# One weight load cut by partitions, and vector work spread over three engines, in a decode step that streams 91 MB

## The chip, the cores and the metric

One core of a Trainium2 chip. The metric is device time in microseconds. The kernel before takes 220.0 us (median of three runs, 219.9 to 220.01).

## The reference

One decode step for two sequences (B = 2). Grouped-query attention with 32 query heads over 8 key/value heads looks at the last W = 4096 positions of the caches; beside it runs a dense layer with the Mish activation; a sigmoid gate mixes the two. Everything is float32.

```python
g = sigmoid((x * gate_w).sum(-1))                      # x: [2, 1, 512]
q = x @ wq                                             # wq: 512 x 4096
p = softmax(q k^T * 128 ** -0.5)                       # per head, 4096 positions
a = (p v) @ wo                                         # wo: 4096 x 512
h = x @ w1 + b1                                        # w1: 512 x 1792
b = (h * tanh(softplus(h))) @ w2                       # w2: 1792 x 512
out = g * a + (1 - g) * b
```

## The kernel before

**The stream.** All large data arrives through one DMA queue, issued by SyncE (SP), in the order wq (two loads of 4 MB), w1, then k and v of the eight key/value heads in turn (4 MB each), and last the first ten blocks of w2 (`w2_0`, 2.5 MB), wo in four loads (`wo0`, `wo4`, `wo6`, `wo7`: four, two, one and one heads' worth) and the last four blocks of w2 in three (`w2_10` with two blocks, 512 KB, then `w2_12` and `w2_13` with one each, 256 KB). Each load is a tile of 128 partitions: a row of every partition is one packet, 32 KB for k and v, 4 KB for `w2_10`, 2 KB for `w2_12` and `w2_13`. All but the three last go through the pool `stream` with five buffers (`load`, line 54); those three have tiles of their own (`load_w2`, line 262). A stream load waits on SP until its buffer is free, and what follows it in the queue waits behind it.

**The attention.** TensorE works in column groups of 32: the two queries sit in 32-row blocks (Q = 32), and the four groups j hold four slices of the positions. For each head `softmax` (lines 128 to 144) makes 128x512 scores in `sc`, VectorE takes the row maximum (`mx`, line 134), ScalarE the exponentials with their row sums (`p`, `ls`), TensorE transposes p, and a copy brings it to SBUF (`pT`, line 143). `values` (line 146) multiplies pT with v into `o` and adds its four blocks, weighted by the 0/1 columns of `pick`, into `od` (lines 154 and 156). Each slice keeps its own maximum; only after the last head does `weights` (line 159) find the common one, turn the differences into factors (`ms`, lines 163 to 175), and make `kf` (factors by slice and head) and `r` (gate over the sum). `outputs` (line 194) then multiplies od with kf and writes the scaled, transposed heads to `oT`.

**The dense layer.** `hidden` (line 203) computes h early, after the queries, and the Mish in 14 small vector operations and one exponential, into `actT`.

**The end.** `project` (line 278) accumulates `w2_0` and wo into `acc`, in the four column groups: the columns of the result are the same in all groups, so that they must still be added. After the last wo pass ScalarE copies the left half of `acc` to `asum`, VectorE the right half (lines 306 and 307). `finish` (line 288) collects the result in `fin`: the two blocks of `w2_10` (`output(1)`), `asum` folded over its four groups by the matrix `fold`, then `w2_12` and `w2_13`. VectorE copies fin to `res` and SP stores it (lines 319 and 320).

A float32 matmul appears in the trace as two passes, each with a weight load. The framework (Tile) sets semaphores and buffers, and may put independent instructions of an engine in another order than the source.

## Time and profile before

| | |
|---|---|
| median of three runs | 220.0 us |
| profiled execution | 219.93 us, of which the span is 218.1 us |
| granted TensorE clock, mean | 0.797 |
| read from HBM | 91.24 MB, 419 GB/s over the span |
| TensorE busy (passes, weight loads) | 131.8 us, 39.3 us |
| VectorE, ScalarE, POOL busy | 36.2, 8.6, 3.0 us |
| VectorE instructions | 131 |

The span begins with the first instruction and ends with the last; the rest of the 219.93 us lies around it. Rows of a timeline have start, duration, engine, source line, operation, tiles and count, and in brackets the idle time before with what ended it. Rows of a table by stretch have, per engine, busy time and count, in the order PE, PEld, DVE, ACT, POOL; then the granted clock, the mean busy share of the 16 DMA engines and GB/s. A group's row has busy time and mean ns of one.

### The profile page before, as it was taken

To read this page: it belongs to the slowest core of one execution; us is meant where nothing else is said; L and a number is where in the kernel's file an instruction comes from. 1 tells how busy PE (TensorE), PEld (TensorE's weight loads), DVE (VectorE), ACT (ScalarE), POOL (GpSimd) and SP (SyncE) were. 2 spreads that over 40 slices of the span, in tenths; PEclk is the share of its full clock that TensorE was granted. 3 is DMA by queue.
4 is the path that set the end of the run, shared out by engine and by line. 5 is a ranking of instruction groups with operands and counts; after the bars stand their busy time and mean duration, and the time that the engine had idled before them with its cause. 6 is when DMAs were issued, how large, how long until landed. Compare 5 with 4: busy or idle time off the path is not lost.

```text
span 218.1 us, 1883 instructions
## 1 busy us (share of the span) xinstructions
PE 131.8 (60%) x798; PEld 39.3 (18%) x798; DVE 36.2 (17%) x131; ACT 8.6 (4%) x21; POOL 3.0 (1%) x9
## 2 busy tenths in 40 slices
PE   0057637295763828435684937467394946496975
PEld 0012212012111201201121112112021211341222
DVE  1012112402202021120112012011202023503001
ACT  2000000001001000100100010010001001000000
POOL 5000000000000000000000000000000000000000
PEclk9999988766669696995858787885858579758799
DMA  7998999999999999999999999999999999999993
GB/s 288 391 477 385 442 430 466 397 464 403 463 403 463 406 457 403 463 403 463 403 460 403 463 409 457 415 457 409 454 409 457 409 457 399 439 433 436 413 408 117
DMA packets 4183, 91.41 MB, mean 419 GB/s; under 512 B 592, under 2 KB 720, under 8 KB 1104
## 3 DMA queue, kind: packets, MB, share of 16 engines
q1 hardware_dynamic: 4176, 91.31, 97.6%
q8 instruction: 6, 0.10, 0.2%
q14 instruction: 1, 0.01, 0.0%
HBM read 91.24 MB, written 0.07 MB: 419 GB/s over the span
## 4 chain that ended last, share of the span: by engine, by line
DMA 80%; PE 16%; DVE 1%; SPq 1%; issue 1%; ACT 1%; DVEq 0%
DMA k<-in_kt 40%; DMA w<-in_w 20%; DMA v<-in_v 20%; PE o L150 5%; PE sc L131 5%; PE hp L209 2%; PE ol L196 1%; PE fin L288 1%; SPq L54 1%; ACT p L138 0%; PE lp L186 0%; DVE mx L134 0%; DVE pT L143 0%; PE pp L142 0%; DVE r L189 0%
## 5 line engine op out<-in xcount | busy, mean ns | idle before, releaser
L131 PE MATMUL sc<-k,qz 128*32 128x512 f32 x256 | 44.9, 866 | 32.2 <-DMA k<-in_kt 32.2
L150 PE MATMUL o<-v,pT 128*32 128x512 f32 x256 | 46.1, 886 | 10.2 <-DMA v<-in_v 8.4
L131 PEld LDWEIGHTS sc<-k,qz 128*32 128x32 f32 x256 | 10.1, 152 | 66.9 <-DMA k<-in_kt 39.6
L150 PEld LDWEIGHTS o<-v,pT 128*32 128x32 f32 x256 | 11.9, 153 | 38.0 <-issue 32.7
L134 DVE TENSOR_REDUCE mx<-sc 128x1 f32<-128x512 f32 x8 | 5.5, 692 | 63.1 <-PE sc L131 63.1
L113 PE MATMUL qp<-wqa,x 128*32 128x512 f32 x32 | 6.2, 710 | 13.3 <-DVE xg L93 13.3
L142 PE MATMUL pp<-ident,p 128*128 128x128 f32 x32 | 5.5, 295 | 14.4 <-ACT p L138 14.4
L154 DVE TENSOR_SCALAR od<-o,pick 128x128 f32<-128x128 f32 x8 | 2.8, 351 | 51.2 <-PE o L150 51.2
L138 ACT ACTIVATE p<-sc,bias 128x512 f32<-128x512 f32 x8 | 5.5, 687 | 140.2 <-DVE bias L136 122.7
L278 PE MATMUL acc<-wo,oT 128*32 128x512 f32 x64 | 8.8, 614 | 1.7 <-DMA wo<-in_wo 1.7
L156 DVE SCALAR_TENSOR_TENSOR od<-o,pick,od 128x128 f32<-128x128 f32 x24 | 8.4, 351 | 0.9
L143 DVE COPY pT<-pp 128x512 f32<-128x512 f32 x8 | 5.5, 692 | 11.7 <-PE pp L142 11.7
L142 PEld LDWEIGHTS pp<-ident,p 128*128 128x128 f32 x32 | 3.4, 142 | 21.1 <-ACT p L138 21.1
L209 PE MATMUL hp<-w,x 128*32 128x512 f32 (+1 forms) x32 | 5.0, 730 | 3.4 <-DMA w<-in_w 3.4
L196 PE MATMUL ol<-kf,od 128*128 128x8 f32 x16 | 3.5, 351 | 2.3 <-DVE od L156 1.6
L278 PE MATMUL acc<-w,actT 128*32 128x512 f32 x20 | 4.5, 914 | 0.0
L113 PE MATMUL qp<-wqb,x 128*32 128x512 f32 x32 | 3.6, 594 | 1.3 <-DMA wqb<-in_wq 1.3
L113 PEld LDWEIGHTS qp<-wqa,x 128*32 128x32 f32 x32 | 1.2, 128 | 15.7 <-DVE x L80 13.3
L196 PEld LDWEIGHTS ol<-kf,od 128*128 128x128 f32 x16 | 3.4, 312 | 3.5 <-DVE od L156 2.6
L278 PEld LDWEIGHTS acc<-wo,oT 128*32 128x32 f32 x64 | 2.4, 113 | 7.2 <-issue 5.6
L307 DVE COPY asum<-acc 128x256 f32<-128x256 f32 x1 | 0.4, 425 | 13.6 <-ACT asum L306 13.6
L116 DVE COPY qs<-qp 128x512 f32<-128x512 f32 x2 | 1.4, 692 | 7.7 <-PE qp L113 7.7
(75 smaller groups left out, 33.3 us busy)
## 6 DMA issues: line engine op xcount, KB each, us to landing
k<-in_kt SPq DMA_DIRECT2D x8, 4096.0 KB, 42.2
v<-in_v SPq DMA_DIRECT2D x8, 4096.0 KB, 43.0
wqa<-in_wq SPq DMA_DIRECT2D x1, 4096.0 KB, 12.2
wqb<-in_wq SPq DMA_DIRECT2D x1, 4096.0 KB, 21.0
wo<-in_wo SPq DMA_DIRECT2D x1, 4096.0 KB, 38.4
w<-in_w SPq DMA_DIRECT2D x1, 3584.0 KB, 29.1
w<-in_w SPq DMA_DIRECT2D x1, 2560.0 KB, 38.6
wo<-in_wo SPq DMA_DIRECT2D x1, 2048.0 KB, 33.3
```

The lines of the kernel that those rows point to most:

```text
L113: nc.tensor.matmul(qp[Q * k : Q * k + Q, :], x32[:, c, :], w[:, c, k, :], start=(c == 0), stop=(c == DC - 1))
L131: nc.tensor.matmul(sc[Q * j : Q * j + Q, :], qz[:, kv, m * Q : m * Q + Q], t[:, (m * NJ + j) * 512 : (m * NJ + j + 1) * 512], start=(m == ...
L134: nc.vector.tensor_reduce(mx[:, kv : kv + 1], sc, axis=AX.X, op=ALU.max)
L138: nc.scalar.activation(p, sc, AF.Exp, bias=bias, scale=SCALE, accum_out=ls[:, kv : kv + 1])
L142: nc.tensor.transpose(pp[:, c, :], p[:, c * P : (c + 1) * P], ident)
L143: nc.vector.tensor_copy(pT, pp)
L150: nc.tensor.matmul(o[Q * j : Q * j + Q], pT[:, c, Q * j : Q * j + Q], t[:, (c * NJ + j) * 512 : (c * NJ + j + 1) * 512], start=(c == 0), s ...
L154: nc.vector.tensor_scalar_mul(d, o[:, 0, :], pick[:, 0:1])
L156: nc.vector.scalar_tensor_tensor(d, o[:, m, :], pick[:, m : m + 1], d, op0=ALU.mult, op1=ALU.add)
L196: nc.tensor.matmul(ol[:, kv].rearrange("p b h -> p (b h)"), od[:, kv, :], kf[:, kv, :], start=True, stop=True)
L209: nc.tensor.matmul(hp[Q * j : Q * j + Q, :n], x32[:, c, :], w[:, c, j * FG * P : j * FG * P + n], start=(c == 0), stop=(c == DC - 1))
L278: nc.tensor.matmul(acc[Q * j : Q * j + Q, :], lhsT, rhs, start=(n_col[j] == 0), stop=(n_col[j] == n - 1))
```

## The change

`w2_10` is loaded in three DMAs of 81, 32 and 15 partitions instead of one of 128. [...] The three last w2 tiles get a pool of their own, `ends`, placed behind `stream`, which is now the first pool and starts at a multiple of 1024 bytes (`res` is padded for it).

VectorE's program becomes shorter, 47 instructions by the title:

- the constants and the spread x (`fold`, `key`, `ones`, `x32`), the products for the gate, two of its steps, most of the Mish and the last factor of `r` move to POOL;
- the copies of `qs`, `pT`, `ms` and `hs` move to ScalarE, and the scale goes into the copy of qs, so that the maximum can be stored negated and used as the bias of the exponential at once;
- many small operations become one over a larger pattern (`qz`, `mj`, `h`, the subtraction in `weights`, the product in `outputs`);
- `values` gathers two heads in one PSUM tile and makes od for both with one product and one sum;
- the Mish becomes h * e(e + 2) / (e(e + 2) + 2) with e = exp(min(h, 20));
- the sum over the gate's four chunks goes into TensorE's accumulation, four matmuls for one.

Since od now comes in pairs, the first `outputs` covers six heads instead of seven and the second two instead of one. `pT` has one buffer instead of two, and `o` takes two PSUM banks.

The diff, cut to its core:

```diff
+CAP = 20.0
 CUTS = (0, 10, 12, 13, 14)
+PARTS = (0, 81, 113, 128)
...
+    stream = ctx.enter_context(tc.tile_pool(name="stream", bufs=5))
+    ends = ctx.enter_context(tc.tile_pool(name="ends", bufs=1))
     const = ctx.enter_context(tc.tile_pool(name="const", bufs=1))
-    stream = ctx.enter_context(tc.tile_pool(name="stream", bufs=5))
+    single = ctx.enter_context(tc.tile_pool(name="single", bufs=1))
...
-        xs = const.tile([P, B], F32, name="xs")
-        nc.vector.tensor_reduce(xs, xg.rearrange("p c b -> p b c"), axis=AX.X, op=ALU.add)
         zp = ps_1.tile([P, B], F32, tag="q", name="zp")
-        nc.tensor.matmul(zp, ones, xs, start=True, stop=True)
+        for c in range(DC):
+            nc.tensor.matmul(zp, ones, xg[:, c, :], start=(c == 0), stop=(c == DC - 1))
...
-        nc.vector.tensor_reduce(mx[:, kv : kv + 1], sc, axis=AX.X, op=ALU.max)
-        bias = tiny.tile([P, 1], F32, tag="bias", name=f"bias{kv}")
-        nc.vector.tensor_scalar_mul(bias, mx[:, kv : kv + 1], -SCALE)
+        nc.vector.tensor_reduce(mx[:, kv : kv + 1], sc, axis=AX.X, op=ALU.max, negate=True)
         p = work.tile([P, 512], F32, tag="p", name=f"p{kv}")
-        nc.scalar.activation(p, sc, AF.Exp, bias=bias, scale=SCALE, accum_out=ls[:, kv : kv + 1])
+        nc.scalar.activation(p, sc, AF.Exp, bias=mx[:, kv : kv + 1], accum_out=ls[:, kv : kv + 1])
...
-        nc.vector.tensor_copy(pT, pp)
+        nc.scalar.copy(pT, pp)
...
-        d = od[:, kv, :]
-        nc.vector.tensor_scalar_mul(d, o[:, 0, :], pick[:, 0:1])
-        for m in range(1, BN):
-            nc.vector.scalar_tensor_tensor(d, o[:, m, :], pick[:, m : m + 1], d,
-                                           op0=ALU.mult, op1=ALU.add)
+        if kv % 2:
+            ...
+            nc.vector.tensor_tensor(
+                ov, pair[0].rearrange("p k (m d) -> p k m d", m=BN),
+                pick[:, None, :, None].to_broadcast([P, 2, BN, DH]), op=ALU.mult)
+            nc.vector.tensor_reduce(od[:, kv - 1 : kv + 1], ov.rearrange("p k m d -> p k d m"),
+                                    axis=AX.X, op=ALU.add)
...
-        for j in range(NJ):
-            for n in range(NH):
-                nc.vector.tensor_tensor(m4[:, j, :, n, :], m4[:, j, :, n, :], top, op=ALU.subtract)
-        nc.scalar.activation(ms, ms, AF.Exp, scale=SCALE)
+        for n in range(NH):
+            nc.gpsimd.tensor_tensor(m4[:, :, :, n, :], m4[:, :, :, n, :],
+                                    top[:, None].to_broadcast(mj.shape), op=ALU.subtract)
+        nc.scalar.activation(ms, ms, AF.Exp, scale=-1.0)
...
+        nc.gpsimd.tensor_scalar_min(e, h, CAP)
+        nc.scalar.activation(e, e, AF.Exp)
+        nc.gpsimd.tensor_tensor(ho, h, omg[:, None, :].to_broadcast([P, FC, B]), op=ALU.mult)
+        nc.gpsimd.tensor_scalar_add(nu, e, 2.0)
+        nc.gpsimd.tensor_tensor(nu, nu, e, op=ALU.mult)
+        nc.gpsimd.tensor_scalar_add(de, nu, 2.0)
+        nc.vector.reciprocal(de, de)
+        nc.gpsimd.tensor_tensor(nu, nu, de, op=ALU.mult)
+        nc.gpsimd.tensor_tensor(actT[:, :, ::RS], nu, ho, op=ALU.mult)
...
-        t = const.tile([P, (f1 - f0) * D], F32, name=f"w2_{f0}")
-        nc.sync.dma_start(t, src)
+        t = ends.tile([P, (f1 - f0) * D], F32, name=f"w2_{f0}")
+        cuts = PARTS if i == 1 else (0, P)
+        for p0, p1 in zip(cuts, cuts[1:]):
+            nc.sync.dma_start(t[p0:p1], src[p0:p1])
         return t
...
-    outputs(ol, kf, r, 0, HKV - 1)
+    outputs(ol, kf, r, 0, HKV - 2)
     values(HKV - 1, pT, last_v)
...
-    outputs(ol, kf, r, HKV - 1, HKV)
+    outputs(ol, kf, r, HKV - 2, HKV)
...
-    res = nc.alloc_sbuf_tensor("res", [P, P], F32).ap()
+    start = -(-nc.sbuf_base // 32) * 8
+    res = nc.alloc_sbuf_tensor("res", [P, P + (-start - P) % 256], F32).ap()[:, :P]
```

## The prediction

> **What bounds the kernel now.** First the page: the totals, the share of the transfers and the chain that ended last.

> ```profile
> span 218.1 us, 1883 instructions
> PE 131.8 (60%) x798; PEld 39.3 (18%) x798; DVE 36.2 (17%) x131; ACT 8.6 (4%) x21; POOL 3.0 (1%) x9
> DMA  7998999999999999999999999999999999999993
> q8 instruction: 6, 0.10, 0.2%
> q14 instruction: 1, 0.01, 0.0%
> DMA 80%; PE 16%; DVE 1%; SPq 1%; issue 1%; ACT 1%; DVEq 0%
> ```

> The DMA engines are full in all slices but the first and the last. VectorE works 17% of the span and is no bound, so shorter vector work pays only where something waits for it at the end. Seven packets of instructions, six of about 16 KB and one of 8 KB, travel on the same engines as the weights. So the end has to be read finely: the busy share of the DMA engines, first in a steady stretch, then in steps of 0.2 us.

> ```profile
> 70.00:80.00 10.00, 5.34 (x32) 1.59 (x32) 1.53 (x5) 0.00 (x0) 0.00 (x0) 0.83 0.99 424
> 213.20:213.40 0.20, 0.20 (x4) 0.08 (x7) 0.00 (x0) 0.00 (x0) 0.00 (x0) 1.00 0.98 389
> 213.60:213.80 0.20, 0.20 (x8) 0.00 (x0) 0.00 (x0) 0.00 (x0) 0.00 (x0) 1.00 0.48 184
> 213.80:214.00 0.20, 0.20 (x4) 0.00 (x0) 0.00 (x0) 0.00 (x0) 0.00 (x0) 1.00 0.42 164
> 214.60:214.80 0.20, 0.20 (x15) 0.19 (x8) 0.15 (x1) 0.02 (x1) 0.00 (x0) 1.00 0.39 154
> 215.00:215.20 0.20, 0.20 (x8) 0.07 (x8) 0.07 (x1) 0.00 (x0) 0.00 (x0) 1.00 0.06 21
> 215.20:215.40 0.20, 0.20 (x10) 0.20 (x12) 0.00 (x0) 0.00 (x0) 0.00 (x0) 1.00 0.00 0
> ```

> The last two columns are the DMA share and GB/s. The share falls from 0.98 to 0.48 at 213.6 and stays near 0.4 until 214.8: 0.39 to 0.48 of 16 engines is six to eight engines still at work for more than a microsecond after the others ran dry. Seven late engines and seven instruction packets fit each other (my inference; no view names an engine). One engine moves 424 / 16 = 26.5 GB/s, so a row of 4 KB takes 0.155 us on it.

> Now the end. The timeline, with the landing times of the last loads (issue plus time to landing):

> ```profile
> L54 SPq DMA_DIRECT2D wo<-in_wo x4: 327/328/328, 164.8 to 198.9; - x4
> DMA to landing us min/median/max: 14.1/30.5/38.4
> L262 SPq DMA_DIRECT2D w<-in_w x3: 424/425/432, 199.2 to 200.2; - x3
> DMA to landing us min/median/max: 15.0/15.2/15.3
> 213.12 1.07 PE L278 MATMUL acc<-wo,oT 128*32 128x512 f32 x8 [1.34 <-DMA wo<-in_wo]
> 214.24 0.37 ACT L306 COPY asum<-acc 128x256 f32<-128x256 f32 x1 [27.26 <-PE acc L278]
> 214.28 0.64 PE L288 MATMUL fin<-w,actT 128*32 128x128 f32 x16
> 214.65 0.42 DVE L307 COPY asum<-acc 128x256 f32<-128x256 f32 x1 [13.55 <-ACT asum L306]
> 215.13 0.11 PEld L288 LDWEIGHTS fin<-asum,fold 128*32 128x32 f32 x2 [0.26 <-DVE asum L307]
> 215.57 0.16 PEld L288 LDWEIGHTS fin<-w,actT 128*32 128x32 f32 x8
> 215.28 0.72 PE L288 MATMUL fin<-w,actT 128*32 128x128 f32 x14
> 216.06 0.29 DVE L319 COPY res<-fin 128x128 f32<-128x128 f32 x1 [0.99 <-PE fin L288]
> ```

> Two chains reach the last matmul almost together. Chain A: the last wo load lands at 198.9 + 14.1 = 213.0, its eight matmul passes end at 214.19, ScalarE copies half of acc until 214.61, VectorE the other half from 214.65 to 215.07, and from 215.13 TensorE has 20 passes left (4 for the second half of asum, 8 for w2_12, 8 for w2_13). Chain B: the last w2 load lands at 200.2 + 15.3 = 215.5 and its eight weight loads start at 215.57. Both end at 216.00; the copy of res starts at 216.06.

> **The change, part by part.**

> *The load in parts.* w2_10, 128 rows of 4 KB, is eight rows on each engine now. After it nine engines carry twelve, six carry three and one carries two. If the seven light engines are the seven late ones, they shed 5 x 0.155 = 0.78 us (the sixteenth 0.93), and the other nine gain 4 x 0.155 = 0.62 us. Late engines then land near 215.5 - 0.78 = 214.7. The early ones ran dry at 213.6 and by the late ones' lag between last packet and landing (215.2 to 215.5, 0.3 us) landed at 213.9; they go to about 214.5, or 214.6 with the two further DMAs' completions. So chain B's landing moves from 215.5 to about 214.7: 0.8 us earlier. What is late next is chain A, which this part does not touch: the last wo load stands ahead of w2_10 in SP's queue, with its rows spread as before.

> What chain A leaves of the 0.8 us: without chain B's wait, TensorE goes from 215.13 through 20 passes. The row at 214.28 has 16 passes in 0.64 us, 0.16 us for each four when the first four have 0.16 too, so 20 need 0.75 to 0.80 and end at 215.88 to 215.93, against 216.00. Bounds: 0 gained (the passes already follow each other) to 0.12. I take 0.1, nearest to the row.

> SP issues two more DMAs at 0.43 us each: w2_12 and w2_13 are queued behind them and go out 0.9 us later, at 200.6 and 201.1. One of the last may also have to wait on SP for an earlier load whose semaphore it takes up; the store, 15 us later, is all that stands behind. Their data is wanted by the engines only after the last wo load, at 213.0, so 12 us cover this. TensorE has three landings to await in place of one ahead of output(1); that work has until 214.65 (the first half of asum) and the parts land by about 213.6. Cost 0; with the cover gone, a wait of some 0.05 us each.

> [...] No run here shows an engine's number yet.

> *VectorE's shorter program.* One instruction packet falls in this stretch on the queue that has only one in all:

> ```profile
> DMA packets 165, 4.53 MB, mean 453 GB/s; under 512 B 26, under 2 KB 26, under 8 KB 26
> q14 instruction: 1, 0.01, 0.2%
> 0.00:45.00 45.00, 19.87 (x126) 6.22 (x130) 8.20 (x48) 1.68 (x3) 3.00 (x9) 0.92 0.97 412
> ```

> It comes between 40 and 50 us, when VectorE has begun 48 of its 131 instructions. I take it for VectorE's, and that a program of 47 does without it. That frees one engine of the seven of 8 KB, 0.31 us at 26.5 GB/s; the other six, twice the size and on another queue, I take for TensorE's, whose 1596 entries no other engine comes near; they stay (the gate's three more small matmuls add 12 entries). The end waits for the latest engine, so this part gives 0, bounds 0 to 0.1.

> [...]

> *Vector work spread over ScalarE and POOL.* While data streams all of this is covered: k and v land 42 to 43 us after issue. It counts only from the last k on, and there against TensorE's slack before chain A.

> ```profile
> 210.71 1.07 PE L278 MATMUL acc<-wo,oT 128*32 128x512 f32 x8 [0.34 <-DMA wo<-in_wo]
> 183.03 0.69 DVE L134 TENSOR_REDUCE mx<-sc 128x1 f32<-128x512 f32 x1 [6.75 <-PE sc L131]
> 186.23 0.41 DVE L172 TENSOR_TENSOR ms<-ms,top 8x16 f32<-8x16 f32 x4
> 189.40 3.16 PE L196 MATMUL ol<-kf,od 128*128 128x8 f32 x14 [0.65 <-DVE r L189]
> 200.44 0.39 PE L196 MATMUL ol<-kf,od 128*128 128x8 f32 x2 [1.64 <-DVE od L156]
> 199.26 1.12 DVE L156 SCALAR_TENSOR_TENSOR od<-o,pick,od 128x128 f32<-128x128 f32 x3
> L143 DVE COPY pT<-pp 128x512 f32<-128x512 f32 x8 | 5.5, 692 | 11.7 <-PE pp L142 11.7
> L82 POOL MEMSET qz<- 128x1152 f32 x1 | 1.1, 1062 | 0.0
> L359 POOL MEMSET const-float32-1.0<- 128x1 f32 x1 | 0.1, 98 | 0.0
> ```

> TensorE waits for wo data for 0.34 us and 1.34 us (chain A's first row) before the last eight wo passes: 1.68 us of slack. The weights chain runs from 183.0 to 189.4. It loses VectorE's eight subtractions (0.8 us for two rows like that at 186.23), three of four maxima and a few copies; it gains two subtractions on POOL, each between the smallest and the largest POOL row, 0.1 to 1.06 us, and a copy on ScalarE behind the exponential. Net -1.4 to +0.6; I take -0.4, as 8x64 elements are nearer to the small row. The first outputs group has 12 passes instead of 14, -0.45 us. After the last values, od now comes for two heads from a product and a sum over 1024 columns: 0.692 us for 512 and 0.29 for 128 (the res copy) give 1.04 ns a column, so 1.2 us each, 2.45 us against four steps of 0.35, or +1.05, and two more output passes +0.4. Together +0.6, bounds -0.8 to +1.6, all below 1.68. So 0 on the end; beyond that it is paid in full.

> *The order of the buffers in SBUF.* Nothing in the profile prices it; the first row of the steady stretch is full already. I take 0, and +-0.3 us as the bound, a tenth of a percent of the stream either way.

> **The sum.** Profiled execution: 219.93 us, span 218.1, 0.07 below the 220.0 median of the runs. -0.1 for chain A's remainder, 0 for the rest: 219.8 on the profile's time, 219.9 on the median. Own range 219.6 to 220.2. A difference of 0.2%, 0.44 us, is about what a measurement of this kernel can tell from none.

> **The rivals.**

> *Faster: the last w2 passes get ahead of asum.* If TensorE's program has w2_12 and w2_13 before the second half of asum, only 4 passes follow 215.13, 16 fewer at 0.16 for four, and the end moves from 216.00 to about 215.4: 219.4 us. For it: those loads would land by 214.7, 0.4 us before asum is ready. Against: in this trace the order is that of the source, and the source keeps it. 14%, a faster chain A for some other cause included.

> *Slower: the light engines are not the late ones.* One mechanism: a late engine among the nine heavy ones lands at 215.5 + 0.62 + 0.1 = 216.2, TensorE's last eight loads start at 216.27 instead of 215.57, and everything after follows: +0.7, 220.6 us. It decides as soon as one of the six latest is heavy. For it: no view names engines. Against: nine early and seven late is just the split that the change makes. 13%.

> *Slower: TensorE overruns its slack.* POOL's subtractions near 1.06 us each and the od wait in full, and a few tenths more than the bound: +0.3, 220.2 us; 4%.

> *Slower: the 81 rows collide.* Two engines that write through one way into the memory would each need twice 9 x 0.155 us, +1.4 for the nine, which then land at 215.9 instead of 214.5 and pass chain A: +0.4, 220.4 us; 4%. [...]

> **How the numbers follow.** No change 65%, faster 14%, the heavy late engine 13%, overrun and collision 8%. Faster by over 0.2% then has 0.15, slower by over 0.2% has 0.18 (the heavy late engine and most of the collision), within 0.2% has 0.67. The range goes to the faster rival at 219.4 and the heavy late engine at 220.7.

> **What would show it.** Right: the DMA share falls from about 1 to 0 within some 0.6 us around 214.2 instead of standing at 0.4; only six instruction packets are left; the last eight fin passes no longer wait for w2, and the chain of waits ends in ScalarE's and VectorE's copies of acc, still near 215.07. TensorE still waits for the last wo load. Wrong: a share of 0.5 or more up to 215.8 (the heavy engines end it), no wait for wo before the last eight passes (TensorE overran), or a wo landing well before 213.0 (chain A was not fixed after all).

## The result, and the profile after

The changed kernel takes 222.4 us (median of four runs, 222.12 to 222.88) against 219.97 us for the kernel before (four runs beside them): 1.0105 of its time, 95% interval 1.0082 to 1.0128. The forecast was no change, 219.9 us in a range of 219.4 to 220.7. The profiled execution took 222.12 us, 2.19 more than the one before; its span grew by 2.1. Two executions among the experiments below, of 364.67 us (`e8_extra_shared`) and 231.27 us (`e11_program_heads`), were in a slower state and are left out of the ratios.

First the page of the kernel after: the totals, and what is left of the packets of instructions.

```profile
span 220.2 us, 1835 instructions
PE 128.0 (58%) x804; PEld 39.4 (18%) x804; DVE 22.1 (10%) x34; ACT 15.3 (7%) x34; POOL 7.5 (3%) x29
q8 instruction: 6, 0.10, 0.2%
```

VectorE's busy time fell from 36.2 to 22.1 us (34 instructions, where the title of the change has 47), and the 8 KB packet on the other queue is gone. Neither shows in the time. Where the time went stands in the stretches before the end, in the same columns as in the prediction (the last three: granted clock, DMA share, GB/s).

```profile
70.00:80.00 10.00, 5.30 (x32) 1.33 (x32) 3.11 (x2) 0.00 (x0) 0.00 (x0) 0.83 0.97 418
212.00:212.20 0.20, 0.20 (x6) 0.02 (x4) 0.00 (x0) 0.00 (x0) 0.00 (x0) 1.00 1.07 266
213.20:213.40 0.20, 0.20 (x6) 0.00 (x0) 0.00 (x0) 0.00 (x0) 0.00 (x0) 1.00 0.78 195
213.60:213.80 0.20, 0.20 (x4) 0.00 (x0) 0.00 (x0) 0.00 (x0) 0.00 (x0) 1.00 0.78 215
215.20:215.40 0.20, 0.20 (x4) 0.00 (x0) 0.00 (x0) 0.00 (x0) 0.00 (x0) 1.00 0.85 266
216.60:216.80 0.20, 0.00 (x1) 0.03 (x1) 0.00 (x0) 0.00 (x0) 0.00 (x0) 1.00 0.16 61
211.50:214.00 2.50, 2.50 (x22) 0.50 (x12) 0.00 (x0) 0.00 (x0) 0.00 (x0) 1.00 0.96 225
```

The last row's counterpart in the kernel before:

```profile
211.50:214.00 2.50, 1.16 (x12) 0.19 (x8) 0.00 (x0) 0.00 (x0) 0.00 (x0) 1.00 0.87 347
```

Read share and GB/s side by side. Before, they go together: share 0.98 with 389 GB/s at 213.2, share 0.48 with 184 at 213.6. After, the engines are busy (0.96 from 211.5 to 214) and move 225 GB/s instead of 347. Busy engines that move less have slower packets here, as the trace shows: a 4 KB row of w2_10 took 159 ns before, all 128 of them (one 160); after, the median is 247 and the longest 374 ns. Nineteen 8 KB rows of the last wo load took 452 to 628 ns instead of 309.

Now the end of the kernel after, first its timeline.

```profile
207.22 6.85 PE L282 MATMUL acc<-wo,oT 128*32 128x512 f32 x54
214.53 1.06 PE L282 MATMUL acc<-wo,oT 128*32 128x512 f32 x8 [0.46 <-DMA wo<-in_wo]
215.66 0.37 ACT L310 COPY asum<-acc 128x256 f32<-128x256 f32 x1 [27.88 <-PE acc L282]
216.06 0.42 DVE L311 COPY asum<-acc 128x256 f32<-128x256 f32 x1 [12.83 <-ACT asum L310]
216.80 0.65 PE L292 MATMUL fin<-w,actT 128*32 128x128 f32 x16 [1.21 <-DMA w<-in_w]
217.72 0.16 PEld L292 LDWEIGHTS fin<-w,actT 128*32 128x32 f32 x8
218.22 0.29 DVE L323 COPY res<-fin 128x128 f32<-128x128 f32 x1 [1.73 <-PE fin L292]
```

The rows of the DMA issues, for wo and then for the blocks of w2; landing is issue plus time to landing.

```profile
L57 SPq DMA_DIRECT2D wo<-in_wo x4: 327/327/328, 164.6 to 198.8; - x4
DMA to landing us min/median/max: 15.7/31.1/38.6
L266 SPq DMA_DIRECT2D w<-in_w x5: 320/377/424, 199.2 to 203.2; - x5
DMA to landing us min/median/max: 14.5/16.7/16.9
```

And the chain of work that ended last: start, duration, what.

```profile
199.96 16.70 DMA w<-in_w
216.66 0.14 issue
216.80 1.40 PE fin L292 x40
218.19 0.02 issue
218.22 0.29 DVE res L323
```

Both chains of the prediction came later. Chain A: the last wo load lands at 198.8 + 15.7 = 214.5 instead of 213.0, and the copies of acc end at 216.48 instead of 215.07. Chain B: the last part of w2_10 lands at 216.66, the last w2 load at 203.2 + 14.5 = 217.7 instead of 215.5. TensorE starts on w2_10 at 216.80, and the eight weight loads of the last w2 block start at 217.72, as soon as it has landed; before, they started at 215.57. The copy of res starts at 218.22 instead of 216.06, 0.5 us behind chain B's last landing in both kernels. So chain B sets the end, and its 2.16 us are the whole difference. Chain A is late too, but its copies, ready at 216.48, aren't waited for: TensorE only takes them up after the passes on w2_10.

### The profile page after: what moved, and what is told of

The parts are those of the page before. It is cut to its first block, busy times and chain, and to the rows that moved or that the text cites. A ratio compares the mean times of both kernels' runs of the same rounds, so it can differ in the third digit from the quotient of the medians.

```text
span 220.2 us, 1835 instructions
## 1 busy us (share of the span) xinstructions
PE 128.0 (58%) x804; PEld 39.4 (18%) x804; DVE 22.1 (10%) x34; ACT 15.3 (7%) x34; POOL 7.5 (3%) x29
## 4 chain that ended last, share of the span: by engine, by line
DMA 79%; PE 13%; another core or an unknown queue 3%; DVE 1%; SPq 1%; issue 1%; ACT 1%; POOL 0%; POOLq 0%
DMA k<-in_kt 39%; DMA w<-in_w 21%; DMA v<-in_v 19%; PE sc L136 5%; PE o L157 5%; PE ol L202 1%; PE fin L292 1%; SPq L57 1%; ACT p L141 0%; SPq L266 0%; DVE mx L139 0%; PE lp L193 0%; POOL ms L181 0%; DVE r L196 0%
## 5 line engine op out<-in xcount | busy, mean ns | idle before, releaser
L136 PE MATMUL sc<-k,qz 128*32 128x512 f32 x256 | 45.6, 877 | 38.1 <-DMA k<-in_kt 38.1
L157 PE MATMUL o<-v,pT 128*32 128x512 f32 x256 | 38.1, 748 | 13.5 <-DMA v<-in_v 13.5
L157 PEld LDWEIGHTS o<-v,pT 128*32 128x32 f32 x256 | 10.5, 132 | 35.5 <-issue 30.8
L118 PE MATMUL qp<-wqa,x 128*32 128x512 f32 x32 | 7.0, 819 | 13.4 <-POOL x L86 13.4
L141 ACT ACTIVATE p<-sc,mx 128x512 f32<-128x512 f32 x8 | 5.5, 688 | 130.3 <-DVE mx L139 130.3
L214 PE MATMUL hp<-w,x 128*32 128x512 f32 (+1 forms) x32 | 6.5, 895 | 2.9 <-DMA w<-in_w 2.9
L164 DVE TENSOR_TENSOR om<-o,pick 128x1024 f32<-128x1024 f32 x4 | 4.9, 1225 | 30.9 <-PE o L157 30.9
L167 DVE TENSOR_REDUCE od<-om 128x256 f32<-128x1024 f32 x4 | 7.5, 1885 | 0.1
L146 ACT COPY pT<-pp 128x512 f32<-128x512 f32 x8 | 4.7, 586 | 6.2 <-PE pp L145 6.2
L214 PEld LDWEIGHTS hp<-w,x 128*32 128x32 f32 x32 | 1.7, 163 | 6.7 <-issue 6.7
```

Of the source, the lines that this page charges most:

```text
L118: nc.tensor.matmul(qp[Q * k : Q * k + Q, :], x32[:, c, :], w[:, c, k, :], start=(c == 0), stop=(c == DC - 1))
L136: nc.tensor.matmul(sc[Q * j : Q * j + Q, :], qz[:, kv, m * Q : m * Q + Q], t[:, (m * NJ + j) * 512 : (m * NJ + j + 1) * 512], start=(m == ...
L141: nc.scalar.activation(p, sc, AF.Exp, bias=mx[:, kv : kv + 1], accum_out=ls[:, kv : kv + 1])
L146: nc.scalar.copy(pT, pp)
L157: nc.tensor.matmul(o[Q * j : Q * j + Q], pT[:, c, Q * j : Q * j + Q], t[:, (c * NJ + j) * 512 : (c * NJ + j + 1) * 512], start=(c == 0), s ...
L164: nc.vector.tensor_tensor(ov, pair[0].rearrange("p k (m d) -> p k m d", m=BN), pick[:, None, :, None].to_broadcast([P, 2, BN, DH]), op=ALU ...
```

## The experiments

The theory: the parts of w2_10 make the rows of several engines get in each other's way at the memory. The rivals: only the number of rows on each engine counts, with a late engine among the heavy ones; or it is VectorE's program, through a late TensorE.

### One half of the change at a time

The change with the load whole (`e1_program_alone`):

```diff
-PARTS = (0, 81, 113, 128)
+PARTS = (0, 128)
```

> The changed kernel with w2_10 in one load of 128 partitions again. Theory: the 2.4 us have two sources. The load in parts slows the transfers of the end (GB/s 176 to 262 at a full DMA share from 211.5 to 214 us), and besides it the vector program makes TensorE late: it waited 3.28 us for od after the last values and its wo passes ran without a pause until 214.07. With the load whole the last wo load should land near 213.0 again, but TensorE gets to its passes about 0.9 us after that instead of at once: 220.9 us, 220.5 to 221.3. Rival, the parts alone cost the time: 219.9 us, the last wo passes start within 0.15 us of the landing. Rival, the vector program costs it all: above 222.

The kernel before with the parts alone (`e2_parts_alone`):

```diff
+PARTS = (0, 81, 113, 128)
...
-        nc.sync.dma_start(t, src)
+        cuts = PARTS if i == 1 else (0, P)
+        for p0, p1 in zip(cuts, cuts[1:]):
+            nc.sync.dma_start(t[p0:p1], src[p0:p1])
```

> The kernel before with the one change that w2_10 comes in parts of 81, 32 and 15 partitions. Theory: packets of engines that write into the same part of the memory take up to twice their time, so that the last wo load lands 1.2 to 1.5 us later and the last w2 load about 2 us later: 221.9 us, 221.3 to 222.6, with GB/s under 270 at a DMA share near 1 for some 2 us. Rival, late engines among the nine heavy ones and nothing else: wo lands at 213.0 as before, the last w2 0.7 us later, 220.7 us. Rival, the parts do no harm: 219.9 us.

Measured: the program alone 219.91 us, ratio 0.9994 (0.9977 to 1.001); the parts alone 223.24 us, ratio 1.014 (1.0116 to 1.0165). The load carries all of the loss, and both expectations missed: the 220.9 of the first was too much, the 221.9 of the second (at most 222.6) too little. Without the rest of the change the load costs even more: 3.2 us instead of 2.4.

The first has a point that the median hides. The profiled execution of the program alone took 220.49 us, and its timeline is this:

```profile
201.87 1.02 PE L202 MATMUL ol<-kf,od 128*128 128x8 f32 x4 [3.28 <-DVE od L167]
209.45 5.32 PE L282 MATMUL acc<-wo,oT 128*32 128x512 f32 x44
215.88 0.70 PE L292 MATMUL fin<-w,actT 128*32 128x128 f32 x14
```

TensorE waits 3.28 us for od, and its wo passes then run to 214.77 without any wait for data, where they ended at 214.19 before. In that execution TensorE overran its slack by 0.58 us. A lower clock adds to it: the granted clock is 0.50 from 200.8 to 207.4 there, and in the kernel before it is 0.50 only from 201.3 to 204.7 and then 1.00, so that the first 18 passes behind od took 4.48 us instead of 3.96. Half of the ten runs lie at 219.91 or below, so the overrun is not paid in those.

### Do equal rows on every engine help?

Halves of 64 partitions (`e3_halves`, `PARTS = (0, 64, 128)` in the edit above) are to give each of 16 engines four rows twice; in the kernel after, the part of 32 partitions and the loads of 128 have 16 completions alike. Halves by columns (`e4_columns`) give two DMAs as well, but each over all 128 partitions:

```diff
-        nc.sync.dma_start(t, src)
+        cuts = (0, D, 2 * D) if i == 1 else (0, D)
+        for c0, c1 in zip(cuts, cuts[1:]):
+            nc.sync.dma_start(t[:, c0:c1], src[:, c0:c1])
```

> The kernel before with w2_10 in two loads, partitions 0 to 63 and 64 to 127: four and four rows on each of the 16 engines, so no engine carries more than before. Theory of the collision (each half goes to half of the ways into the memory, two engines to one): w2_10 takes about 1.3 us longer, and late engines on wo are slowed: 221.0 us, 220.6 to 221.6, and GB/s drops near half at a full DMA share. Rival, only the uneven number of rows hurts: one more completion, 220.0 us, 219.9 to 220.2.

> Control: the kernel before with w2_10 in two loads of all 128 partitions, one for each block, 2 KB a row. The bytes of each engine and of each partition are as before, only the number of DMAs and packets grows. Theory of the collision: no more than one further completion on each engine and 8 more packets, 220.0 us, 219.9 to 220.2. Rival, a further DMA on the queue is what costs: 0.3 us or more, 220.3 us and up.

Measured: 223.12 us, ratio 1.0136 (1.0103 to 1.0168), for the halves by partitions; 220.02 us, ratio 0.9994 (0.9974 to 1.0014), for those by columns. The 221.0 expected of the first (at most 221.6) was too little. A stretch of each, first the halves by partitions:

```profile
212.00:212.50 0.50, 0.00 (x0) 0.00 (x0) 0.00 (x0) 0.00 (x0) 0.00 (x0) 1.00 1.03 188
```

and by columns:

```profile
212.50:213.00 0.50, 0.00 (x0) 0.00 (x0) 0.00 (x0) 0.00 (x0) 0.00 (x0) 1.00 1.04 402
```

Full share in both, 188 GB/s in the one and 402 in the other; over 211.5 to 214 the halves by partitions move 175 GB/s at a share of 0.97. The median 4 KB row takes 312 ns there instead of 159. That is close to twice the time, and the rate is close to half (188 of 402 GB/s); that two engines share a way into the memory there is the theory's reading, and no view shows such a way. By that count of rows no engine has one more than another in the halves by partitions, and they lose 3.1 us: uneven rows aren't needed for the loss. A second DMA costs nothing either (220.02 us). What is left is into which partitions several engines write at the same time; the next two runs test it.

### The same rows from the same place, into other partitions

One further load of eight rows of 8 KB, which nothing reads, goes between the last wo load and w2_10: into partitions 0, 4, ..., 28 (`e7_extra_own`) or 0 to 7 (`e8_extra_shared`, `extra[0:8]`). I count one row for each of eight engines, since the probe of 8 partitions below has eight completions; the first expectation calls them 0 to 7, numbers that no view shows.

```diff
+    extra = const.tile([P, 2048], F32, name="extra")
+    nc.sync.dma_start(extra[0:32:4], w2[: 8 * 2048].rearrange("(p x) -> p x", p=8))
```

> [...] Theory of the collision: the row costs its engine 0.31 us and a completion, and no packet is slowed; if a late engine is among 0 to 7 the end moves by about 0.35 us: 220.3 us, 220.0 to 220.5. Rival, any load on fewer than 16 engines is slow by itself: as much as the next run.

> [...] Theory of the collision: the rows take about four times as long, 1.2 us instead of 0.31, so that the end moves by 1.2 to 1.5 us: 221.4 us, 221.0 to 222.0. Rival, the partitions do not matter: the same time as the run before.

Measured: 220.11 us, ratio 1.0002 (0.9981 to 1.0023), and 221.17 us, ratio 1.0034 (1.0015 to 1.0053). By the ratio the second costs 0.75 us. Its median stands higher because five of its nine runs lie at 221.17 to 221.34 and four at 220.45 to 220.65; the kernel before has such an upper group too, 5 of 18 runs, some 0.9 us above the rest. So the 221.4 expected fits the median, and by the ratio it was too much. No run shows the four times that it took for the rows; the longest 4 KB packet below took 3.1 times its 159 ns. The two intervals overlap; its lowest run, 220.45, stands above seven of the ten runs of the first (219.89 to 220.22), and the packets below tell the two apart plainly. One stretch of the load in partitions 0, 4, ..., 28:

```profile
212.50:213.00 0.50, 0.00 (x0) 0.00 (x0) 0.00 (x0) 0.00 (x0) 0.00 (x0) 1.00 0.97 385
```

and two of the load in partitions 0 to 7:

```profile
212.50:213.00 0.50, 0.00 (x0) 0.00 (x0) 0.00 (x0) 0.00 (x0) 0.00 (x0) 1.00 1.13 320
213.00:213.50 0.50, 0.00 (x0) 0.03 (x1) 0.00 (x0) 0.00 (x0) 0.00 (x0) 1.00 0.90 246
```

With partitions four apart no packet was slowed (309 ns for 8 KB, 159 for 4 KB, 84 for 2 KB), but for one of 8 KB with some 0.8 us, which the kernel before has too. With partitions 0 to 7, 8 further packets of 8 KB, 39 of 4 KB and 44 of 2 KB took over 1.1 times as long, one of 4 KB 495 ns. What is read is the same, and so are the number and the size of the rows; only the partitions written differ.

### Which engines are late?

Three small loads behind the last w2 load, of 4, 8 and 12 partitions with rows of 512 bytes, which nothing reads (`e5_probe`, and once more as `e6_probe_again`):

```diff
+    for n in (4, 8, 12):
+        seen = const.tile([P, P], F32, name=f"seen{n}")
+        nc.sync.dma_start(seen[:n], w2[: n * P].rearrange("(p x) -> p x", p=n))
```

> A probe of where the late engines stand: the kernel before with three further small loads behind w2_13, of 4, 8 and 12 partitions and 512 bytes a row, which nothing reads. [...] Time 220.0 us, 219.9 to 220.4.

> The same probe once more, to see whether the late engines are the same in another execution. If their places are fixed, the counts of late completions in the loads of 4, 8 and 12 repeat; if they are drawn anew, at least one count differs. I expect them to repeat. Time 220.0 us, 219.9 to 220.4.

Measured: 219.88 and 219.87 us in one run each. The trace has 4, 8 and 12 completions for the three loads, in us:

```
e5  4: 213.86 214.04 214.09 | 215.20
    8: 213.88 214.05 214.05 214.22 214.27 | 215.34 215.38 215.47
   12: 214.07 to 214.44 (6) | 215.30 to 215.67 (6)
e6  4: 213.84 213.89 213.91 | 214.78
    8: 213.96 to 214.09 (5) | 214.96 215.36 215.57
   12: 214.04 to 214.26 (6) | 215.14 to 215.76 (6)
```

One late completion of 4, three of 8, six of 12, the same twice; a load of 128 partitions has seven of 16. The three parts have 9, 16 and 15 completions, and I take each for one engine's. If the loads use nested sets of engines, the nine of the 81-partition load among them, three or more of these nine are late. The 81-partition load itself shows late ones: in the kernel after, seven of its nine completions came from 213.64 to 214.17 and two at 215.92 and 216.24; in the kernel with the parts alone six came by 213.92 and three from 215.44 to 216.13. And three completions of the second part had come by 212.38 after the change, before the first of the 81 partitions at 213.64, so three of the light engines were early. The late seven aren't the light seven. And the two completions at the end of each later load stand apart as well: in the last w2 load fourteen engines were through by 216.50, two at 217.62 and 217.68. By their order these are the two late heavy ones (an inference).

The growing counts (one, three, six) fit nested sets, but no view numbers an engine, so which ones a load takes isn't shown.

### Why the load costs more without the rest of the change

In the kernel with the parts alone TensorE waits for the last wo load, and the eight passes behind the wait are slow, by its timeline:

```profile
214.38 1.94 PE L281 MATMUL acc<-wo,oT 128*32 128x512 f32 x8 [2.67 <-DMA wo<-in_wo]
```

and its stretches inside the wait show the clock (third column from the end):

```profile
213.20:213.40 0.20, 0.00 (x0) 0.00 (x0) 0.00 (x0) 0.00 (x0) 0.00 (x0) 1.00 0.86 174
213.60:213.80 0.20, 0.00 (x0) 0.00 (x0) 0.00 (x0) 0.00 (x0) 0.00 (x0) 0.78 0.97 205
213.80:214.00 0.20, 0.00 (x0) 0.00 (x0) 0.00 (x0) 0.00 (x0) 0.00 (x0) 0.50 1.05 205
```

The granted clock falls to 0.5 two microseconds into the wait, and 1.06 us of passes become 1.94. To test it, twelve matmuls whose result nothing reads keep TensorE at work through that wait (`e9_parts_busy`); the parts alone were run again beside it (`e10_parts_again`).

```diff
+            for i in range(12):
+                h = i % NJ
+                nc.tensor.matmul(busy[Q * h : Q * h + Q, :], oT[:, i, :],
+                                 wos[2][2][:, h * D : (h + 1) * D], start=True, stop=True)
```

> The parts alone, with 12 further matmuls on TensorE between the passes of wo6 and those of the last wo, whose result nothing reads. With the parts alone TensorE waited 2.67 us for the last wo; from 213.9 its granted clock was 0.5, and the last eight wo passes took 1.94 us instead of 1.07. Theory: the idle wait costs the clock, which is why the parts alone cost more (223.2 us) than the whole change (222.4), whose late TensorE had no such wait. With TensorE kept at work the passes should take 1.07 us and the time fall by 0.8 to 1.2 us, to 222.2 us, 221.9 to 222.6. Rival, the clock is not set by the wait: 223.2 us, passes still 1.9 us.

> The parts alone once more, beside the run before on the same chip: 223.2 us, 222.9 to 223.6, the last wo passes at a clock of 0.5 in 1.9 us; nine completions of the 81-partition load, three of them late.

Measured: 222.09 us, ratio 1.0084 (1.0058 to 1.011), with the work; 223.23 us, ratio 1.0136 (1.0113 to 1.0159), without. The timeline with it:

```profile
211.39 2.76 PE L308 MATMUL busy<-wo,oT 128*32 128x512 f32 x24
214.53 1.06 PE L281 MATMUL acc<-wo,oT 128*32 128x512 f32 x8 [0.39 <-DMA wo<-in_wo]
```

and that of the parts alone, run again:

```profile
214.46 1.94 PE L281 MATMUL acc<-wo,oT 128*32 128x512 f32 x8 [2.90 <-DMA wo<-in_wo]
```

The data lands at the same time (214.40 and 214.32), the passes take 1.06 us instead of 1.94, and the kernel 1.1 us less. So the loss of 3.2 us is 2.1 from the load itself and 1.1 from the clock. The whole change doesn't pay the second part, because its TensorE comes late from od and is busy until 214.07.

### Does od by heads give a gain?

The change with the load whole and od made by head again, in four steps, with outputs for seven heads and one as before (`e11_program_heads`), so that TensorE isn't late:

```diff
-PARTS = (0, 81, 113, 128)
+PARTS = (0, 128)
...
-        if kv % 2:
-            ...
+        d = od[:, kv, :]
+        nc.vector.tensor_scalar_mul(d, o[:, 0, :], pick[:, 0:1])
+        for m in range(1, BN):
+            nc.vector.scalar_tensor_tensor(d, o[:, m, :], pick[:, m : m + 1], d,
+                                           op0=ALU.mult, op1=ALU.add)
```

> The candidate for the best version: the changed kernel with w2_10 in one load and od made for each head by the four steps of the kernel before (first outputs over seven heads). It keeps VectorE's shorter work elsewhere and the aligned tiles, and does without the wait of 3.28 us for od, which made TensorE late in some executions of the program alone (219.72 to 220.71). Theory: 219.8 us, no execution above 220.2, TensorE waits for wo before the last passes. Rival, the pairs did not matter: 219.9 us with the same spread.

Measured: 219.95 us, ratio 0.9993 (0.9978 to 1.0008), with runs at 220.22 and 220.96, so that the expected ceiling of 220.2 didn't hold. By its timeline the wait for od is 1.64 us again and the wo passes wait for data:

```profile
198.62 0.39 PE L194 MATMUL ol<-kf,od 128*128 128x8 f32 x2 [1.64 <-DVE od L159]
213.00 1.07 PE L274 MATMUL acc<-wo,oT 128*32 128x512 f32 x8 [1.44 <-DMA wo<-in_wo]
```

That is no gain over the pairs (219.91) and none over the kernel before, some of whose runs reached 221.08 beside it. In this execution the granted clock stayed at 1.00 from 198 to 207.4, so its wait for wo can't be put down to od alone. What the 0.58 us of the one late execution are worth over many runs stays open: it is too small to tell from that spread. No kernel here beats the one before.

## Why the prediction was wrong

**The step that failed: "a row of 4 KB takes 0.155 us", whatever partitions it is written to.** From it the prediction had the load in parts bring chain B's last landing from 215.5 to 214.7. It came at 217.7, and that set the end. With the load whole all 128 packets took 159 ns (one 160), late engines or not, so there none slowed another. Cut in parts, the median row took 247 ns. The cause that the runs point to is several engines that write at once into neighbouring partitions: eight rows into partitions 0 to 7 slowed packets (one of 4 KB to 495 ns), the same rows into 0, 4, ..., 28 didn't. The rows that the sums give each engine (twelve, three and two) fit the 9, 16 and 15 completions of the parts; which engines these are no run shows.

**The second half of the step: the light engines were to be the late ones.** That was the assumption, and it was wrong for at least two of the nine heavy ones. The rival for this, at 13%, had its sign right: late heavy engines end the load of 81 partitions, at 215.92 and 216.24. Its price, +0.7, was under a third of the loss, since it took 155 ns for each row and the trace has 247 in the median.

**Chain A, "which this part does not touch".** This was wrong too, though it didn't set the end. The reason given was that the last wo load stands ahead of w2_10 in SP's queue. But engines run dry one by one: in the kernel after, completions of the last wo load came from 211.14 to 214.48, and those of w2_10's second part from 211.96 on. So an early engine writes w2_10 while a late one still writes its rows of wo, and both were slow (247 ns for 159 in the median, nineteen rows of wo 452 to 628 ns for 309). So wo landed 1.5 us later (214.5 for 213.0). In the kernel with halves it landed at 199.1 + 15.9 = 215.0, by the rows of its issues:

```profile
L55 SPq DMA_DIRECT2D wo<-in_wo x4: 327/328/328, 164.3 to 199.1; - x4
DMA to landing us min/median/max: 15.9/30.1/39.0
```

**The rival of the collision, 4% and +0.4 us.** The sign was right and the term mis-sized. No run shows two engines on one way into the memory, or the twofold time that the term took from it; what they showed is slower rows for loads of fewer partitions, 312 ns for 159 in the halves and 247 in the three parts. The twofold time is more than the median packet took after the change (1.55 times) and less than the longest (374 ns). But the rival put it on the nine heavy engines' own rows alone, 1.4 us on engines that were taken to be early, and left the late ones their 215.5. The late ones are the ones that set the end, and they were slowed in wo as well as in w2_10: +2.2 us on chain B. How the +2.2 divides between slow packets and more rows on the heavy late engines isn't settled. But halves, with even rows by my count, cost 3.1, and taking off 1.1 for the clock (the eight passes took 1.94 us there too) leaves 2.0 without any heavy engine, against 2.4 for the whole change. This is an estimate: the 1.1 was measured with the other parts.

**SP's two more DMAs, and the three landings.** Two DMAs for one by columns cost nothing (220.02 us). In the kernel after, SP did wait for an earlier load (2.4 us for wo) before the last w2, as the prediction allowed: five issues span 199.2 to 203.2. The data was wanted 10 us after. The parts of w2_10 were to land by about 213.6 and landed by 216.66; TensorE waited for them until 216.80, which is chain B's delay again.

**The packet of instructions.** Right: it vanished, six are left, and it gave nothing. With the load whole and this packet gone (`e1_program_alone`) six engines are late instead of seven, and the end still waits for the latest.

**The vector program.** Bounded right in the median, with a wrong size inside. These are the groups of the od pair in the kernel after:

```profile
L164 DVE TENSOR_TENSOR om<-o,pick 128x1024 f32<-128x1024 f32 x4 | 4.9, 1225 | 30.9 <-PE o L157 30.9
L167 DVE TENSOR_REDUCE od<-om 128x256 f32<-128x1024 f32 x4 | 7.5, 1885 | 0.1
```

The product took 1.225 us, as taken; the sum 1.885 instead of 1.2, where the price came from rows over contiguous columns and this sum runs along a strided axis (the likely reason, not tested). So the od wait rose by 1.64 us to 3.28, and with the two more output passes and the lower clock TensorE stood at the edge of its slack of 1.68 us or over it. That slack was itself read from one execution, with the clock at 0.50 from 201.3 to 204.7. Alone, that is no change in the median, and 0.58 us in one profiled execution. Together with the late wo load it costs nothing: TensorE still waited 0.46 us for wo. There its lateness even hid the fall of the clock (1.00 from 207.7 on).

**The end.** The predicted order held: the copies of acc came after the last wo pass and TensorE kept the order of the source, so the faster rival didn't come about. Two signs named as signs of being wrong came: a share of 0.85 at 215.2, named as the mark of heavy engines that end it, and a wo landing that moved, though later and not earlier.

## What to carry to other kernels

Time a cut by partitions before building on it: here it slowed the load's own rows (247 ns for 159) and rows of the load ahead of it (452 to 628 ns for 309), and cost 3.2 us alone, while a cut by columns cost nothing (220.02 us). Read the DMA share beside GB/s: here a share of 0.96 with 225 GB/s, where the kernel before moved 347 at 0.87, went with slow packets, and a share of 0.48 with 184 GB/s, at 84 and 159 ns a packet, with engines that had run out of work. And before rows are moved away from late engines, probe for them: small loads over 4, 8 and 12 partitions, put last in the queue, had one, three and six late completions here.
